# A spectral mixing layer with a two-layer MLP: two more Strassen blocks, a new order inside a Strassen pair, and transform pieces that share ticks

## The chip, the cores and the metric

The kernel runs on one core of a Trainium2 chip. A core has five engines with a queue each: TensorE (PE, matrix products; its weight loads are shown as PEld), VectorE (DVE), ScalarE (ACT), GpSimd (POOL) and SyncE (SP, which issues transfers). Products land in PSUM, eight banks of 128 x 512 float32; ACT and DVE take them out. The metric is the device time of one launch in microseconds (us), the median of the runs.

## The reference, cut to what matters

x is 4 batches of 3008 rows and 256 columns. The output is y = irfft(shrink(rfft(x) W + b)) along the rows, W complex 256 x 256, followed by an MLP over all 12032 rows: silu(y w_in) w_out with 2048 hidden columns.

```
X = np.fft.rfft(x, axis=1)
Yr = Xr @ w_r - Xi @ w_i + b_r ;  Yi = Xr @ w_i + Xi @ w_r + b_i
Yr = sign(Yr) * max(|Yr| - 0.01, 0)      (Yi likewise)
y = np.fft.irfft(Yr + 1j*Yi, n=3008, axis=1)
h = y @ w_in ;  out = (h / (1 + exp(-h))) @ w_out
```

## The kernel before, in words

A DFT of 3008 = 47 x 64 rows is made as two matrix products with a twiddle table between them. Per batch there is a first stage (over the 47; a result of 24 row pairs), a second stage with the mixing product and the shrink (12 steps, each of two rows of the 24), an inverse first stage, and an inverse second stage that makes the rows of the MLP blocks. Between stages the data goes through DRAM (`scr1`, `scr2`).

The MLP works in 24 blocks of 512 rows (the last of 256), and in a block over 16 hidden slices of 128. One hidden slice of one block is a **tick**: `mlp1` makes the hidden slice transposed (six float32r products of 128 x 512: high and low parts of both operands), ACT applies silu and rounds the high part `gh`, DVE makes the low part `gl`, and four **units** (`mlp2`, L675: one 128 x 512 and one 128 x 256 product each) add the slice to the four output accumulators. The units of a tick run two ticks later. PSUM has four accumulators, two banks `h` for `mlp1`, and two banks `d0` and `d1` that everything else takes in turn.

In the blocks of `FAST` (13 to 22) two ticks make a **pair**: the 2x2 form of Strassen-Winograd needs seven half products (three matmuls of 128 x 256 each, `fast_product`, L608) in place of eight. `fast_one` starts a pair in the even tick, `fast_more` goes on in the odd tick, `fast_two` ends it in the next even tick, after the next pair's `fast_one`. A pair holds two banks, `px` and `py`, out of three. `fast_bank` hands a bank out again only when its readers are done.

The transforms of batches 1 to 3 lie between: each tick can hold one transform step, run after `mlp1` and ahead of the tick's units. A planner in plain Python (L930 to L998) gives each step a tick number. The steps are: `i2` and `i2_ends` (inverse second stage of a block, three ticks per block, one PSUM bank); `u3_step` (**U**: the even halves run second stage `s2_3` and inverse first stage `i1`, the odd halves the mixing product `mix3`; two banks each); and for batches 2 and 3 the first stage in 16 pieces (**S**), each in two parts. `stack_split` (L247) rounds 1024 columns of x to `sx` (ACT, L250) and makes the rest in the upper rows (DVE, L251), one buffer; `stack_product` (L254) runs two products of 128 x 512 into two banks (L260), and per bank ACT copies the low half (L261) and DVE adds it (L262). The order of the steps before the change is written as strings of U and S; a split stands up to two ticks ahead of its product, and never before the product of the piece ahead of it. `fills` (L1005) runs a tick's steps in the order in which they were entered, and then hands stores to SP. Each engine's instructions are issued in program order; semaphores make a reader wait for its writer and a writer for the earlier readers of its buffer.

Of the kernel before, what the change touches and what calls it, by code (L numbers as in the profile page):

```python
# [9 lines left out]
F32 = mybir.dt.float32  # L10
F32R = mybir.dt.float32r
U32 = mybir.dt.uint32
ACTF = mybir.ActivationFunctionType
ALU = mybir.AluOpType
# [4 lines left out]
S, D, DFF, NB = 3008, 256, 2048, 4  # L19
# [7 lines left out]
BLK = 512  # L27
# [5 lines left out]

STACKED = 2

FAST = range(13, 23)

X_BUFS = [0, 1, 2, 3, 4, 5, 6, 0, 1, 2, 3, 4, 0, 2, 1, 0]
BLOCKS = [(c, min(BLK, NT - c)) for c in range(0, NT, BLK)]
# [77 lines left out]
def spectral_mlp_kernel(ctx: ExitStack, tc: tile.TileContext, x, w_r, w_i, b_r, b_i, w_in, w_out, c1, c2, c3, c4, c3f, c5, out):  # L117
    nc = tc.nc
# [21 lines left out]
    tl = None  # L140
# [20 lines left out]
    def flush(n):  # L161
        for dst, src in stores[:n]:
            nc.sync.dma_start(out=dst, in_=src)
        del stores[:n]
# [311 lines left out]
    def i2(i, e):  # L476
# [10 lines left out]
        h, l = xt[i]  # L487
        if i in FAST and e == 0:
            xf[i] = tl.tile([128, 2, BLK], F32, tag="xf", bufs=1, name="xf")
        split_x(i, p[:, q], (slice(None), e, q))  # L490

    def split_x(i, v, q):
        h, l = xt[i]
        nc.scalar.copy(h[q], v)
        if i in FAST:
            nc.scalar.copy(xf[i][q], v)
# [58 lines left out]
    HB = BLK // 2  # L555
    xf, th, tw, fast = {}, {}, {}, []
# [51 lines left out]
    def fast_product(p, i, q, a, b, begins):  # L608

        w = [v[:, a, :] for v in tw[q]] if isinstance(a, int) else \  # L610
            [v[:, a[0], q * 256 + a[1] * 128:q * 256 + a[1] * 128 + 128] for v in win]
        m = [v[:, b, :] for v in th[i]] if isinstance(b, int) else \
            [v[:, b[0], b[1] * HB:(b[1] + 1) * HB] for v in xt[i]]
        for n, (j, k) in enumerate(((0, 0), (1, 0), (0, 1))):
            nc.tensor.matmul(  # L615
                out=p, lhsT=w[j], rhs=m[k], start=(begins and n == 0), stop=(n == 2), skip_group_check=True,
            )
# [7 lines left out]
    def fast_one(i, q):  # L625

        px = fast_bank()
        fast_product(px[:, 0:HB], i, q, (0, 0), (0, 0), True)
        fast_product(px[:, HB:BLK], i, q, 0, 0, False)
        u = tl.tile([128, HB], F32, tag="u", bufs=2, name="u")  # L630
        nc.scalar.copy(u, px[:, 0:HB])
        fast.append([i, q, px, u])

    def fast_more():

        i, q, px, u = fast[-1]
        py = fast_bank()
        fast_product(py[:, 0:HB], i, q, 1, 1, True)
        fast_product(py[:, HB:BLK], i, q, 2, 2, False)
        g = tl.tile([128, 4, HB], F32, tag="gp", bufs=3, name="gp")  # L640
        nc.vector.tensor_tensor(out=u, in0=py[:, 0:HB], in1=u, op=ALU.add)
        nc.vector.tensor_tensor(out=g[:, 3, :], in0=px[:, HB:BLK], in1=u, op=ALU.add)  # L642
        nc.vector.tensor_tensor(out=g[:, 3, :], in0=py[:, HB:BLK], in1=g[:, 3, :], op=ALU.add)
        fast[-1] += [py, g]

    def fast_two():

        i, q, px, u, py, g = fast.pop(0)
        fast_product(px[:, 0:HB], i, q, (1, 0), (1, 0), False)
        fast_product(px[:, HB:BLK], i, q, 3, (1, 1), False)  # L650
        fast_product(py[:, HB:BLK], i, q, (1, 1), 3, False)
        nc.scalar.activation(out=g[:, 0, :], in_=px[:, 0:HB], func=ACTF.Silu)  # L652
        nc.vector.tensor_tensor(out=g[:, 2, :], in0=py[:, HB:BLK], in1=u, op=ALU.add)  # L653
        nc.vector.tensor_tensor(out=g[:, 1, :], in0=px[:, HB:BLK], in1=u, op=ALU.add)  # L654
        nc.scalar.activation(out=g[:, 1, :], in_=g[:, 1, :], func=ACTF.Silu)  # L655

        def parts(r):
            h, l = [tl.tile([128, 2, HB], F32R, tag=f"g{k}", bufs=4, name=f"g{k}") for k in "hl"]
            v = g[:, 2 * r:2 * r + 2, :]
            if r:  # L660
                nc.scalar.activation(out=v, in_=v, func=ACTF.Silu)
            nc.scalar.copy(h, v)  # L662
            nc.vector.tensor_sub(l, v, h)  # L663
            gf[i, 2 * q + r] = tuple(a.rearrange("p a c -> p (a c)") for a in (h, l))
            units.extend((i, 2 * q + r, t) for t in range(BLK // 128))

        parts(0)
        later.append(lambda: parts(1))
# [6 lines left out]
    def mlp2(i, f, t):  # L675
# [31 lines left out]
        if i == LAST:  # L707
            (nc.vector.tensor_copy if t % 2 else nc.scalar.copy)(out=o, in_=a[:, 0:D])
        elif i in FAST:
            w = sb.tile([128, 512], F32, tag="g", bufs=3, name="ow")  # L710
# [64 lines left out]
    with tc.manual_schedule():  # L775
# [156 lines left out]
        def at(t, fn, *args):  # L932
            fill.setdefault(t, []).append((fn, args))

        taken = {9, 25} | set(range(33, len(ticks), NFF))

        def put(t, fn, *args):

            while t in taken:
                t += 1  # L940
            taken.add(t)
            at(t, fn, *args)
            return t

        for i in range(1, len(BLOCKS)):
            t = (16 * i - 15 if i in FAST else 16 * i - 9) if i > 1 else -1
            if i > 1:
                at(t, i2_load, i)
            put(t + 2, i2, i, 0)
            put(t + 4, i2, i, 1)  # L950
            t = put(t + 6, i2_ends, i)
            if i in FAST:
                moving = fast_moving(i)
                for k in range(8):
                    at(t + 1 + k, next, moving, None)
                assert t + 8 < 16 * i
# [11 lines left out]
        def turns(b):  # L968

            for u in range(NU + 3):  # L970
                for half in range(2 if 0 < u <= NU else 1):
                    yield b, u, half

        free, stacked = 24, 18
        for b, order in ((1, "U" * 4 + "UUUUSUUUS" * 3 + "UU" + "S." * 10), (2, "UUSUUSUSUS" * 3 + "USUS" + "USU" * 2 + "UUU"), (3, "U" * 27)):
            todo, split = list(turns(b)), 0
            assert order.count("U") == len(todo) and order.count("S") in (0, 16)
            ready = max(free, stacked + 4)
            for k in range(2):
                at(ready - 2 + k, u_load, b, k)  # L980
            for k in order:
                if k == "U":
                    free = put(max(free, ready), u3_step, *todo.pop(0))
                elif k == "S":
                    while free in taken:
                        free += 1
                    at(max(free - 2, stacked), stack_split, b + 1, split)
                    stacked = put(free, stack_product, b + 1, split)
                    split += 1
                last = free  # L990
                free += 1

        def swap_pools():
            nonlocal tl
# [4 lines left out]
        for q in range(NFF // 2):  # L999
            steps = fast_weights(q)  # L1000
            for k in range(3):
                at(last + 2 + q * 8 // 5 + k, next, steps, None)
        assert last + 1 <= 16 * FAST[0] - 13 and last + 2 + 11 + 2 < 16 * FAST[0] + 12

        def fills(t):  # L1005
            for fn, args in fill.pop(t, []):
                fn(*args)
            flush(1 if t < 12 else 4)

        def run(n):  # L1010
            for v in units[:n]:
                mlp2(*v)
            del units[:n]

        def rest_of_pair():
            while later:
                later.pop(0)()

        first_fast, last_fast = 16 * FAST[0], 16 * (FAST[-1] + 1)
        for t in range(len(ticks) + 1):  # L1020
            i, f = ticks[t] if t < len(ticks) else (LAST, None)
            while deferred:
                deferred.pop(0)()
            if t and ticks[t - 1][0] not in FAST:
                split_g(*ticks[t - 1])
            if i in FAST:
                q = t - first_fast
                if f % 2 == 0:
                    state["fast"] = True
                    fast_one(i, f // 2)  # L1030
                    if q != 2:
                        run(2)
                    if q:
                        fast_two()
                        run(2)
                else:
                    run(1)
                    fast_more()
                    if f != 3:
                        rest_of_pair()  # L1040
                    run(1 if q < 4 else 3)
                    rest_of_pair()
                fills(t)
                continue
            if t == last_fast:
                run(2)
                fast_two()
                run(3)
                rest_of_pair()
            if f is not None:  # L1050
                mlp1(i, f)
            fills(t)
            if last_fast <= t < last_fast + 3:
                run(3 if t == last_fast else 4)
            else:
                run(sum(v[:2] != ticks[t - 1] for v in units))
        run(len(units))
        for k, (dst, src) in enumerate(stores):
            eng = nc.scalar if k % 2 else nc.sync
# [28 lines left out]
```

## Time and profile before

| | us |
|---|---|
| median of 3 runs (lowest, highest) | 1353.45 (1353.04, 1359.64) |
| profiled execution, its time | 1355.36 |
| profiled execution, its span | 1353.6 |
| PE busy in the span | 1340.7 (99%) |
| DVE, ACT, POOL busy | 845.2, 800.5, 214.8 |
| transforms end (last inverse step, tick 183) | at about 797 |
| first Strassen block (tick 208) | at 868.5 |

The span runs from the first to the last instruction; the run's time holds the launch as well. PE is busy from the first to the last tick, so its own instructions are read by the distance from one start to the next: a matmul's shown duration overlaps the next one.

### The profile page before, as it was taken

The numbers are of one execution on the slowest core, as the hardware profiler recorded it, in microseconds if no ns is written. First come the engines' busy times: TensorE is split into PE (matmuls) and PEld (weight loads), VectorE is DVE, ScalarE is ACT, GpSimd is POOL, SyncE is SP. The second block draws the span as 40 slices with busy tenths as digits, with TensorE's granted clock in tenths as the row PEclk, the third lists the DMA queues.
The fourth block names the chain that finished last, engine by engine and source line by source line (L and its number), as shares of the span: only waits on it lengthen the run. The fifth ranks groups of instructions, "written<-read, shape, count | busy, mean of one in ns | idle before, by whom it ended". The sixth has DMA issues, their size and how long they took to land.

```text
span 1353.6 us, 22051 instructions
## 1 busy us (share of the span) xinstructions
PE 1340.7 (99%) x8309; PEld 1184.6 (88%) x8309; DVE 845.2 (62%) x1608; ACT 800.5 (59%) x1646; POOL 214.8 (16%) x312
## 2 busy tenths in 40 slices
PE   8999999999999999999999999999999999999998
PEld 4977888888888888888888888899999999999998
DVE  3767757575665767675556656366666666666663
ACT  5546555565676656565554545466666666666665
POOL 2001002121111212121111100122122112212200
PEclk9999999999999999999999999999999999999999
DMA  8876514241434435341433121001100100110001
GB/s 264 260 223 182 137 47 131 73 124 49 121 101 129 120 92 153 76 123 54 119 90 111 50 67 28 7 22 39 28 3 27 40 28 1 28 40 17 1 17 24
DMA packets 72762, 109.85 MB, mean 81 GB/s; under 512 B 8400, under 2 KB 54224, under 8 KB 72656
## 3 DMA queue, kind: packets, MB, share of 16 engines
q1 hardware_dynamic: 58537, 79.07, 20.6%
q0 software_dynamic: 10544, 25.68, 7.4%
q10 hardware_dynamic: 3575, 3.70, 0.9%
q8 instruction: 65, 1.06, 0.3%
q14 instruction: 41, 0.34, 0.1%
HBM read 70.93 MB, written 37.49 MB: 80 GB/s over the span
## 4 chain that ended last, share of the span: by engine, by line
PE 92%; DMA 3%; issue 2%; ACT 1%; DVE 1%; POOL 0%; SPq 0%; DVEq 0%; POOLq 0%; ACTq 0%
PE acc L692 24%; PE h L534 22%; PE h L615 14%; PE acc L696 12%; PE mix L382 6%; PE i L472 3%; PE s L357 2%; PE i L430 2%; PE mix L321 2%; PE s L260 1%; PE acc L687 1%; DMA scr<-s1o 1%; DMA scr<-i1o 1%; PE i2e L472 1%; PE i L427 1%
## 5 line engine op out<-in xcount | busy, mean ns | idle before, releaser
L692 PE MATMUL acc<-wout,gh 128*128 128x512 f32 x1472 | 543.2, 400 | 0.0
L696 PE MATMUL acc<-wout,gl 128*128 128x256 f32 x1472 | 413.0, 281 | 0.2 <-DVE gl L551 0.2
L534 PE MATMUL h<-xt,win 128*128 128x512 f32 (+1 forms) x1344 | 337.5, 386 | 0.0
L692 PEld LDWEIGHTS acc<-wout,gh 128*128 128x128 f32 x1472 | 277.7, 189 | 50.3 <-ACT ww L759 0.3
L541 ACT ACTIVATE g<-h 128x512 f32<-128x512 f32 (+2 forms) x225 | 130.8, 582 | 264.2 <-PE h L534 262.6
L696 PEld LDWEIGHTS acc<-wout,gl 128*128 128x128 f32 x1472 | 278.8, 189 | 4.6 <-DVE gl L551 0.5
L534 PEld LDWEIGHTS h<-xt,win 128*128 128x128 f32 x1344 | 232.2, 188 | 47.2 <-DVE xt L498 0.4
L551 DVE TENSOR_TENSOR gl<-g,gh 128x512 fp32r<-128x512 f32 (+2 forms) x225 | 150.9, 673 | 74.8 <-ACT gh L550 73.5
L663 DVE TENSOR_TENSOR gl<-gp,gh 128x512 fp32r<-128x512 f32 x160 | 117.1, 732 | 102.0 <-ACT gh L662 102.0
L550 ACT CAST gh<-g 128x512 fp32r<-128x512 f32 (+2 forms) x225 | 136.1, 605 | 1.4
L662 ACT CAST gh<-gp 128x512 fp32r<-128x512 f32 x160 | 99.3, 620 | 5.1
L402 DVE TENSOR_TENSOR y<-q,mix 64x256 f32<-64x256 f32 x144 | 60.3, 419 | 58.9 <-PE mix L382 55.0
L389 POOL TENSOR_TENSOR q<-q,bias 128x256 f32<-128x256 f32 x36 | 26.5, 737 | 406.4 <-ACT q L388 406.4
L615 PE MATMUL h<-xt,win 128*128 128x256 f32 x480 | 86.0, 288 | 0.1
L615 PEld LDWEIGHTS h<-xt,win 128*128 128x128 f32 x480 | 68.0, 189 | 7.1 <-DVE gp L642 0.6
L652 ACT ACTIVATE gp<-h 128x256 f32<-128x256 f32 x80 | 30.7, 384 | 73.2 <-PE h L615 73.2
L615 PE MATMUL h<-th,sw_h 128*128 128x256 f32 x240 | 71.0, 296 | 0.5 <-DVE gp L654 0.4
L655 ACT ACTIVATE gp<-gp 128x256 f32<-128x256 f32 x80 | 33.4, 417 | 62.8 <-DVE gp L654 62.8
L653 DVE TENSOR_TENSOR gp<-h,u 128x256 f32<-128x256 f32 x80 | 33.9, 424 | 54.6 <-PE h L615 54.6
L615 PE MATMUL h<-tl,sw_h 128*128 128x256 f32 x240 | 67.8, 282 | 0.0
L615 PE MATMUL h<-th,sw_l 128*128 128x256 f32 x240 | 67.7, 282 | 0.0
L262 DVE TENSOR_TENSOR s1o<-s,s1o 48x512 f32<-48x512 f32 x64 | 41.0, 678 | 32.3 <-ACT s1o L261 32.3
(171 smaller groups left out, 2302.1 us busy)
## 6 DMA issues: line engine op xcount, KB each, us to landing
a<-scr SPq DMA_DIRECT2D x48, 256.0 KB
x_sb<-in_x_dram POOLq DMA_DIRECT2D x64, 188.0 KB, 3.5
gin<-scr SPq DMA_DIRECT2D x30, 384.0 KB
t<-in_c_dram POOLq DMA_DIRECT2D x36, 256.0 KB, 3.1
scr<-i1o SPq DMA_DIRECT2D x36, 256.0 KB
t<-in_c_dram SPq DMA_DIRECT2D x48, 128.0 KB
scr<-s1o SPq DMA_DIRECT2D x32, 192.0 KB
scr<-s1o SPq DMA_DIRECT2D x13, 384.0 KB
```

Source lines behind the costliest of these rows:

```text
L382: nc.tensor.matmul(out=out, lhsT=x_[:, e, c, :], rhs=m[:, e, :], start=(n == 0), stop=(n == 5))
L402: nc.vector.tensor_tensor(out=y[64 * i:64 * i + 64, r, :], in0=q[rows, i, :], in1=pv[rows, i, :], op=op,)
L472: nc.tensor.matmul(out=p[:, o:o + m], lhsT=g_t[b, j // 4][:, q:q + 128], rhs=c4_sb[:, p0:p0 + m], start=True, stop=True,)
L534: nc.tensor.matmul(out=p[:, :n], lhsT=w[:, e, f * 128:(f + 1) * 128], rhs=v[:, e, :n], start=(m == 0), stop=(m == 5),)
L541: nc.scalar.activation(out=g[:, q], in_=p[:, q], func=ACTF.Silu)
L550: nc.scalar.copy(gh[:, q], g[:, q])
L551: nc.vector.tensor_sub(gl[:, q], g[:, q], gh[:, q])
L615: nc.tensor.matmul(out=p, lhsT=w[j], rhs=m[k], start=(begins and n == 0), stop=(n == 2), skip_group_check=True,)
L662: nc.scalar.copy(h, v)
L663: nc.vector.tensor_sub(l, v, h)
L692: nc.tensor.matmul(out=a, lhsT=gh[:, q], rhs=wout[:, f].rearrange("p a c -> p (a c)"), start=begins, stop=False,)
L696: nc.tensor.matmul(out=a[:, D:2 * D], lhsT=gl[:, q], rhs=wout[:, f, 0, :], start=False, stop=ends,)
```

## The change

Blocks 11 and 12 become Strassen blocks too. Inside a pair, the half products change places: `fast_one` makes products 0 and 1, `fast_more` the plain product (0,0) and product 2, `fast_two` product 3 first and then the plain ones; the copy `u` is made in `fast_more`, and the sum that frees `px` follows right behind product 3. The units are laid out otherwise among the calls (`run`), eight per pair as before.

The planner is new. It goes tick by tick, puts an S piece where two or three ticks have passed since the last one and else the next U step, and lets an S piece share a tick with `i2` or `i2_ends`: its product is then entered at tick + 0.5, behind the tick's units. The split of the next piece is entered at whole ticks, at the earliest in the tick of the last product. The last U step moves from tick 183 to tick 162.

```
-FAST = range(13, 23)
+FAST = range(11, 23)
...
     def fast_one(i, q):
         px = fast_bank()
-        fast_product(px[:, 0:HB], i, q, (0, 0), (0, 0), True)
-        fast_product(px[:, HB:BLK], i, q, 0, 0, False)
+        fast_product(px[:, 0:HB], i, q, 0, 0, True)
+        fast_product(px[:, HB:BLK], i, q, 1, 1, False)
...
     def fast_more():
+        i, q, px = fast[-1]
+        py = fast_bank()
+        fast_product(py[:, 0:HB], i, q, (0, 0), (0, 0), True)
+        fast_product(py[:, HB:BLK], i, q, 2, 2, False)
+        nc.scalar.copy(u, py[:, 0:HB])
+        nc.vector.tensor_tensor(out=u, in0=px[:, HB:BLK], in1=u, op=ALU.add)
+        nc.vector.tensor_tensor(out=g[:, 3, :], in0=px[:, 0:HB], in1=u, op=ALU.add)
         nc.vector.tensor_tensor(out=g[:, 3, :], in0=py[:, HB:BLK], in1=g[:, 3, :], op=ALU.add)
...
     def fast_two():
-        fast_product(px[:, 0:HB], i, q, (1, 0), (1, 0), False)
-        fast_product(px[:, HB:BLK], i, q, 3, (1, 1), False)
+        fast_product(px[:, 0:HB], i, q, 3, (1, 1), False)
+        nc.vector.tensor_tensor(out=g[:, 1, :], in0=px[:, 0:HB], in1=u, op=ALU.add)
+        fast_product(py[:, 0:HB], i, q, (1, 0), (1, 0), False)
         fast_product(py[:, HB:BLK], i, q, (1, 1), 3, False)
-        nc.scalar.activation(out=g[:, 0, :], in_=px[:, 0:HB], func=ACTF.Silu)
+        nc.scalar.activation(out=g[:, 1, :], in_=g[:, 1, :], func=ACTF.Silu)
+        nc.scalar.activation(out=g[:, 0, :], in_=py[:, 0:HB], func=ACTF.Silu)
...
+            shared.add(put(t + 2, i2, i, 0))
+            shared.add(put(t + 4, i2, i, 1))
             t = put(t + 6, i2_ends, i)
+            shared.add(t)
...
-        for b, order in ((1, "U" * 4 + "UUUUSUUUS" * 3 + "UU" + "S." * 10), ...
+        while steps:
+            if t not in taken or t in shared:
+                b = steps[0][0]
+                ready = b in stacked and t >= stacked[b] + (3 if b > 1 else 0)
+                apart = 2 if t in shared or not ready else 3
+                if pieces_left and t >= done + apart and pieces_left[0][0] <= b + 1:
+                    at(max(t - 2, done), stack_split, *pieces_left[0])
+                    at(t + 0.5 * (t in shared), stack_product, *pieces_left[0])
+                    done = t
...
+                elif ready and t not in shared:
...
+                    at(t, u3_step, *steps.pop(0))
...
                 if f % 2 == 0:
                     fast_one(i, f // 2)
-                    if q != 2:
-                        run(2)
+                    run(2)
                     if q:
                         fast_two()
-                        run(2)
+                        run(2 if q > 2 else 0)
                 else:
-                    run(1)
                     fast_more()
                     if f != 3:
                         rest_of_pair()
-                    run(1 if q < 4 else 3)
+                    run(2 if q < 4 else 4)
                     rest_of_pair()
...
                 run(sum(v[:2] != ticks[t - 1] for v in units))
+            fills(t + 0.5)
```

Twelve of the 32 S pieces share a tick now (at 41, 43, 45, 57, 59, 61, 91, 93, 105, 107, 109 and 121). On ACT, around the second piece of batch 2 before (tick 42; `gh` and `g` belong to the MLP ticks, `xt` to `i2`, `s1o` to the S piece, `xh` and `xs` to the next U step), the rows are these; the split of this piece stands well ahead, the split of the next one well behind.

```order
L494 CAST xt_2532<-i_2534 128x376 [waits PE_49]
L550 CAST gh<-g 128x512 [waits Activation_49]
L541 ACTIVATE g<-h 128x512 [waits DVE_49,PE_49]
L261 COPY s1o<-s_2563 48x512 [waits PE_49]
L261 COPY s1o<-s_2567 48x512 [waits PE_49]
L550 CAST gh<-g 128x512 [waits Activation_49]
L541 ACTIVATE g<-h 128x512 [waits DVE_49,PE_49]
```

On ACT now, around the same piece (tick 41, then tick 42), the next piece's split `sx` stands between `i2`'s rounding and this piece's two copies.

```order
L494 CAST xt_2532<-i_2534 128x376 [waits PE_49]
L250 CAST sx<-x_sb_72 111x1024 [waits DMASW6_49,DMASW5_49,PE_49]
L261 COPY s1o<-s_2553 48x512
L261 COPY s1o<-s_2557 48x512
L550 CAST gh<-g 128x512 [waits Activation_49]
L541 ACTIVATE g<-h 128x512 [waits DVE_49,PE_49]
L365 CAST xh<-s_2582 128x2x256 [waits PE_49]
```

The split writes the one `sx` buffer, which the piece's two products read; the wait on PE in its row is the one on the second of these products. On DVE now, in the same two ticks, its subtraction stands ahead of the two adds that free the banks.

```order
L551 TENSOR_TENSOR gl<-g,gh 128x512 [waits Activation_49]
L498 TENSOR_TENSOR xt_2533<-i_2534,xt_2532 128x376 [waits Activation_49]
L251 TENSOR_TENSOR sx<-x_sb_72,sx 47x1024 [waits DMASW6_49,Activation_49]
L262 TENSOR_TENSOR s1o<-s_2553,s1o 48x512 [waits Activation_49]
L262 TENSOR_TENSOR s1o<-s_2557,s1o 48x512 [waits Activation_49]
L551 TENSOR_TENSOR gl<-g,gh 128x512 [waits Activation_49]
```

On PE now (end of tick 41, begin of tick 42) the piece stands behind the units, and only the six `mlp1` products lie between it and the next U step, which writes the same two banks.

```order
L692 MATMUL acc<-wout,gh 128x512
L696 MATMUL acc<-wout,gl 128x256
L260 MATMUL s_2553<-sx,c_sb 128x512
L260 MATMUL s_2557<-sx,c_sb 128x512
L534 MATMUL h<-xt_1818,win_83 128x512
L534 MATMUL h<-xt_1818,win_84 128x512
L534 MATMUL h<-xt_1819,win_83 128x512
L534 MATMUL h<-xt_1818,win_83 128x512
L534 MATMUL h<-xt_1818,win_84 128x512
L534 MATMUL h<-xt_1819,win_83 128x512
L357 MATMUL s_2582<-t_2273,a 128x2x64 x4
```

Before, the piece stood ahead of its tick's four units, and `i2` held the next tick. The same order, split ahead of the shared piece's copies and a U step in the tick behind, stands at ticks 41, 43, 57, 59, 91, 105 and 107; at the other five shared pieces no split lies in between.

## Rows read from the trace of the kernel before

**Rows 1.** The page, parts 1 and 2: busy time, granted clock.

```profile
PE 1340.7 (99%) x8309; PEld 1184.6 (88%) x8309; DVE 845.2 (62%) x1608; ACT 800.5 (59%) x1646; POOL 214.8 (16%) x312
PEclk9999999999999999999999999999999999999999
```

**Rows 2.** Waits of PE: line, releaser, us in total, times, longest.

```profile
PE i L472 <- DMA gin<-scr: 3.7, 2, 2.7
```

**Rows 3.** Timeline of PE, ticks and pairs: start, length, what, count.

```profile
854.59 1.55 PE L534 MATMUL h<-xt,win 128*128 128x512 f32 x6
...
865.73 0.63 PE L534 MATMUL h<-xt,win 128*128 128x512 f32 x2
...
1077.07 0.52 PE L615 MATMUL h<-xt,win 128*128 128x256 f32 x3
...
1082.42 0.52 PE L615 MATMUL h<-xt,win 128*128 128x256 f32 x3
...
1093.20 0.52 PE L615 MATMUL h<-xt,win 128*128 128x256 f32 x3
```

**Rows 4.** Timeline at three places where a Strassen product starts late.

```profile
871.97 0.28 PE L615 MATMUL h<-tl,sw_h 128*128 128x256 f32 x1
...
872.30 0.59 PE L615 MATMUL h<-xt,win 128*128 128x256 f32 x3
...
938.31 0.41 DVE L654 TENSOR_TENSOR gp<-h,u 128x256 f32<-128x256 f32 x1
...
938.77 0.39 PE L615 MATMUL h<-th,sw_h 128*128 128x256 f32 x1 [0.21 <-DVE gp L654]
...
939.00 0.28 PE L615 MATMUL h<-th,sw_l 128*128 128x256 f32 x1
...
1319.95 0.28 PE L696 MATMUL acc<-wout,gl 128*128 128x256 f32 x1
...
1320.15 0.61 PE L615 MATMUL h<-xt,win 128*128 128x256 f32 x3
```

**Rows 5.** Groups by line: busy us, mean ns of one, idle before.

```profile
L250 ACT CAST sx<-x_sb 111x1024 fp32r<-111x1024 f32 x32 | 33.6, 1050 | 0.0
L251 DVE TENSOR_TENSOR sx<-x_sb,sx 47x1024 fp32r<-47x1024 f32 x32 | 42.7, 1335 | 27.5 <-ACT sx L250 27.5
L261 ACT COPY s1o<-s 48x512 f32<-48x512 f32 x64 | 34.2, 583 | 0.8
L262 DVE TENSOR_TENSOR s1o<-s,s1o 48x512 f32<-48x512 f32 x64 | 41.0, 678 | 32.3 <-ACT s1o L261 32.3
L631 ACT COPY u<-h 128x256 f32<-128x256 f32 x80 | 30.1, 376 | 22.2 <-PE h L615 21.3
L642 DVE TENSOR_TENSOR gp<-h,u 128x256 f32<-128x256 f32 x80 | 34.0, 424 | 2.7
```

**Rows 6.** Timeline around the first S piece (tick 37).

```profile
227.38 0.62 PE L260 MATMUL s<-sx,c_sb 111*128 111x512 f32 x2
...
227.79 0.60 ACT L541 ACTIVATE g<-h 128x512 f32<-128x512 f32 x1
227.85 0.39 PE L692 MATMUL acc<-wout,gh 128*128 128x512 f32 x1
...
228.42 1.07 ACT L261 COPY s1o<-s 48x512 f32<-48x512 f32 x2
...
229.03 1.28 DVE L262 TENSOR_TENSOR s1o<-s,s1o 48x512 f32<-48x512 f32 x2 [0.41 <-ACT s1o L261]
```

**Rows 7.** Timeline from batch 2's last S piece to its first load.

```profile
416.67 0.63 PE L260 MATMUL s<-sx,c_sb 111*128 111x512 f32 x2
...
419.42 0.30 SPq L163 DMA_DIRECT2D scr<-s1o  x1
...
422.17 0.38 SPq L291 DMA_DIRECT2D a<-scr  x1
```

**Rows 8.** The page, part 6: a load of 256 KB, us to landing.

```profile
t<-in_c_dram POOLq DMA_DIRECT2D x36, 256.0 KB, 3.1
```

More of the change, by code (lines that the diff above doesn't have):

```diff
@@ L627, in fast_one @@
         px = fast_bank()
-        fast_product(px[:, 0:HB], i, q, (0, 0), (0, 0), True)
-        fast_product(px[:, HB:BLK], i, q, 0, 0, False)
-        u = tl.tile([128, HB], F32, tag="u", bufs=2, name="u")
[L631 to L639, printed above, removed]
+        fast_product(px[:, 0:HB], i, q, 0, 0, True)
@@ L640, in fast_more @@
+        fast_product(px[:, HB:BLK], i, q, 1, 1, False)
+        fast.append([i, q, px])
+    def fast_more():
+        i, q, px = fast[-1]
+        py = fast_bank()
+        fast_product(py[:, 0:HB], i, q, (0, 0), (0, 0), True)
+        fast_product(py[:, HB:BLK], i, q, 2, 2, False)
+        u = tl.tile([128, HB], F32, tag="u", bufs=2, name="u")
         g = tl.tile([128, 4, HB], F32, tag="gp", bufs=3, name="gp")
-        nc.vector.tensor_tensor(out=u, in0=py[:, 0:HB], in1=u, op=ALU.add)
-        nc.vector.tensor_tensor(out=g[:, 3, :], in0=px[:, HB:BLK], in1=u, op=ALU.add)
+        nc.scalar.copy(u, py[:, 0:HB])
+        nc.vector.tensor_tensor(out=u, in0=px[:, HB:BLK], in1=u, op=ALU.add)
+        nc.vector.tensor_tensor(out=g[:, 3, :], in0=px[:, 0:HB], in1=u, op=ALU.add)
@@ L643, in fast_more @@
         nc.vector.tensor_tensor(out=g[:, 3, :], in0=py[:, HB:BLK], in1=g[:, 3, :], op=ALU.add)
-        fast[-1] += [py, g]
+        fast[-1] += [u, py, g]
     def fast_two():
         i, q, px, u, py, g = fast.pop(0)
-        fast_product(px[:, 0:HB], i, q, (1, 0), (1, 0), False)
-        fast_product(px[:, HB:BLK], i, q, 3, (1, 1), False)
+        fast_product(px[:, 0:HB], i, q, 3, (1, 1), False)
+        nc.vector.tensor_tensor(out=g[:, 1, :], in0=px[:, 0:HB], in1=u, op=ALU.add)
+        fast_product(py[:, 0:HB], i, q, (1, 0), (1, 0), False)
@@ L651, in fast_two @@
         fast_product(py[:, HB:BLK], i, q, (1, 1), 3, False)
-        nc.scalar.activation(out=g[:, 0, :], in_=px[:, 0:HB], func=ACTF.Silu)
+        nc.scalar.activation(out=g[:, 1, :], in_=g[:, 1, :], func=ACTF.Silu)
+        nc.scalar.activation(out=g[:, 0, :], in_=py[:, 0:HB], func=ACTF.Silu)
         nc.vector.tensor_tensor(out=g[:, 2, :], in0=py[:, HB:BLK], in1=u, op=ALU.add)
-        nc.vector.tensor_tensor(out=g[:, 1, :], in0=px[:, HB:BLK], in1=u, op=ALU.add)
-        nc.scalar.activation(out=g[:, 1, :], in_=g[:, 1, :], func=ACTF.Silu)
@@ L935, in spectral_mlp_kernel @@
         taken = {9, 25} | set(range(33, len(ticks), NFF))
+        shared = set()
         def put(t, fn, *args):
@@ L948, in spectral_mlp_kernel @@
                 at(t, i2_load, i)
-            put(t + 2, i2, i, 0)
-            put(t + 4, i2, i, 1)
+            shared.add(put(t + 2, i2, i, 0))
+            shared.add(put(t + 4, i2, i, 1))
             t = put(t + 6, i2_ends, i)
+            shared.add(t)
             if i in FAST:
@@ L972, in turns @@
                     yield b, u, half
[L974 to L991, printed above, removed]
+        steps = [v for b in range(1, NB) for v in turns(b)]
+        pieces_left = [(b, q) for b in range(STACKED, NB) for q in range(16)]
+        stacked, last, begun = {1: 18}, 24, set()
+        done = 36
+        t = 24
+        while steps:
[7 more added lines that the diff above has]
+                    done = t
+                    if pieces_left.pop(0)[1] == 15:
+                        stacked[max(stacked) + 1] = t
+                elif ready and t not in shared:
+                    if b not in begun:
+                        begun.add(b)
+                        for k in range(2):
+                            at(t - 2 + k, u_load, b, k)
+                    at(t, u3_step, *steps.pop(0))
+                    last = t
+                taken.add(t)
+            t += 1
         def swap_pools():
@@ L1007, in fills @@
                 fn(*args)
-            flush(1 if t < 12 else 4)
+            if t == int(t):
+                flush(1 if t < 12 else 4)
         def run(n):
```

## The prediction

> **What bounds the kernel now.** I read the page's busy shares first, then what PE waited for, then the distances between PE's starts in the timeline. The reader should see in [rows 1] that PE is busy 99% of the span at the full clock, and in [rows 2] that its longest wait in all is 3.7 us, at the start of the first MLP block. So a saving elsewhere is worth nothing unless it removes work or a wait from PE, and every wait put on PE is paid in full. Two yardsticks come from [rows 3]. Four ordinary ticks without a transform take 865.73 - 854.59 = 11.14 us: 2.785 a tick, half of it (1.39) the six products of `mlp1`, half the four units (0.35 each), 5.57 for two ticks. A Strassen pair takes 5.35 (1077.07 to 1082.42) when nothing is late, and 5.39 in the two pairs after it (10.78 to 1093.20).
>
> The 0.04 is a wait that busy time hides. In [rows 4] DVE's sum L654 ends at 938.72, PE starts the next pair's `fast_more` 0.05 later, and the matmul behind that one comes 0.23 after it where 0.12 is usual: a late bank costs the wait and then 0.1 for the restart. Over the ten Strassen blocks I went through the start distances of all L615 matmuls: 63 are longer than usual by 25 ns or more and do not stand behind an inverse piece; together 4.97 us, the first at 871.97 to 872.30, the last at 1319.95 to 1320.15. Most of it is the bank that L654 frees.
>
> **Part 1, two more Strassen blocks.** 16 pairs go from 5.57 to 5.35: 16 x 0.22 = 3.5 us saved, all on PE. The seven products take 21 matmuls at 0.12 = 2.52, against twelve at 1.39 / 6 = 0.232, or 2.78; the rest of the difference is eaten by the units, a little slower in Strassen ticks. What comes with it (the extra copy for the differences, their POOL work, the sums of the weights on DVE) lies in ticks that hold no U step any more, as it did for block 13, where PE shows no wait before 871.97.
>
> The Trainium skill's page "TensorE: Matmul & The Clock Gate", section "Back-to-back issue gap", gives a warm matmul N/2.4 + 2.5 ns, 216 for 512 columns and 109 for 256, so a pair would save 0.30 and the 16 pairs 4.7 us. The rows show 0.232 and 0.12, so the measurement decides; by the page the sum below would be 1.2 us lower.
>
> **Part 2, the order inside a pair.** Before, the bank that `fast_more` takes is freed by the second of two sums behind `fast_two`, with only three units (1.06 us) in between, and that is late again and again. Now product 3 comes first, its sum (0.42, [rows 5]) follows at once, and six matmuls and two units (1.42) lie between product 3's end and the next `fast_more`: drained 0.16 after the next start, plus 0.03, 0.42 and 0.05 makes 0.66, so 0.76 in hand. The new chain is `u`: the copy (0.38) now waits for the plain product in `fast_more`, three sums follow it, and product 3 of the next tick needs the second. On DVE a part's low half (0.7) may stand ahead: about 1.5 us after the end of `fast_more` on PE. Four units, `fast_one`'s six matmuls and two more units last 2.85, so 1.3 in hand. I take 4.5 of the 4.97 as saved. From both sides: all of it and nothing more, 5.0; nothing of it, or a loss of 0.04 in each of 96 pairs (+4), if ACT is late by more than the 1.3 us.
>
> **Part 3, the shared S pieces.** Products, copies, sums and transfers stay the same in number; PE's work does not change. What changes is how close the next user of the two banks stands. An S piece used to have four units and a whole `mlp1` behind it (2.8 us) before the next step's first product; behind the units only `mlp1` is left, 1.39 us. Count from T, the start of `mlp1` behind the piece. In [rows 6] the piece's two products start at 227.38 and end at 228.00, 0.15 after the next matmul's start (227.85). At the five shared pieces without a split, ACT copies the first bank from about T to T + 0.55 (0.58, [rows 5]) and DVE's sum ends near T + 1.26: PE comes at T + 1.39 and finds it free, with 0.1 in hand; the second bank has 0.3. Cost nothing; if that cover goes, up to 0.3 each.
>
> At the other seven (ticks 41, 43, 57, 59, 91, 105, 107) the order in the section on the change puts the next piece's split ahead of the copies on ACT and ahead of the sums on DVE, and this split cannot start before the piece's second product has read `sx`. Then: ACT's cast from T + 0.19 to T + 1.24 (1.05, [rows 5]); DVE's subtraction from T + 1.27 to T + 2.6 (1.34); meanwhile ACT's copies; the first sum from there to T + 3.25 (0.68, less the overlap by which two such sums take 1.28 in [rows 6]); PE 0.05 later, T + 3.3, and 0.1 for the restart [rows 4]. PE had come at T + 1.39: 2.0 us lost. The second sum ends at T + 3.9, before PE has done the 0.7 to 0.8 us of work on the first bank, so it costs nothing more. In each of the seven the next tick holds a U step whose first product takes that bank. 7 x 2.0 = **14.0 us**. From both sides: nothing (if the copies overtook the split), and 2.5 each if the sums were late for PE's second bank too, 17.5. I take 14.0, since each link has a measured length.
>
> Queued behind the waiting cast on ACT are the copies, the `gh` of this tick and the next silu. `gh` is wanted two ticks later and the silu's bank one tick later, so only the two banks are paid for. Behind them on SP is the store of the piece; nothing reads it before the batch's 16 pieces are done.
>
> In the trace ACT keeps its issue order at an S piece: in [rows 6] the first bank was full at about 227.8, but the copy starts at 228.42, behind the silu issued ahead of it (227.79, 0.60 long). The skill's page "PSUM — Partial Sum Buffer", section "Engine vs sequencer instructions", says that the queues of ScalarE and VectorE are strict FIFO. It speaks against this change: by it all seven waits are paid; if a copy could overtake the cast, the time would be the first rival's.
>
> **Part 4, the denser plan.** Batch 2's last piece is now at tick 76 and its first U step at 79, before 88 and 92. In [rows 7] the piece starts at 416.67, its store is issued at 419.42 and the first load at 422.17; [rows 8] has 3.1 us for a load of that size, so it lands 8.6 us after the piece's start, by estimate. From the piece to the U step there are now 0.5 + 1.4 of units, a tick with `i2_ends` (3.3), a tick with a piece (3.3) and 1.4: 9.9 us. Hidden, with 1.3 in hand. The other close neighbours (U after U, unshared S after U, U after S) stand in the old plan too, where no PE wait of any length follows them. I put 0.5 us on this part, between 0 and 3.
>
> **The sum**, on the profiled execution: 1353.6 - 3.5 - 4.5 + 14.0 + 0.5 = 1360.1 for the span. That is +6.5 us; the profiled run's own 1355.36 is 1.9 above the median and I hold that apart, so the median goes from 1353.45 to about **1359.9**.
>
> **Rivals.** (a) The seven waits do not reach PE: the copies go first, or the banks turn out to be other ones. For it: PE's waits in this stretch are nil today. Against it: the order rows and ACT's issue order in [rows 6]. Then 1353.45 - 3.5 - 4.5 = 1345.5, faster. (b) The pair's new order doesn't pay: `u` is on the way of product 3, and where ACT is late by more than 1.3 us (four copies of accumulators at a block's end) PE waits again, as much as it did. Then 1353.45 - 3.5 + 14.0 + 0.5 = 1364.5, slower by 0.8%. For it: the old order's waits cluster where ACT is loaded; against it: margins of 0.76 and 1.3 where the old one was below zero. (c) The split's wait is half covered: DVE takes the sums first or the subtraction overlaps them, and PE waits for the copy alone (cast to T + 1.24, copy 0.5, sum 0.7: T + 2.5, so 1.1 each). Then 1353.45 - 8.0 + 7.7 + 0.5 = 1353.7, no change. Against it the DVE rows.
>
> **How the numbers follow.** What a measurement of this kernel can tell from no change is about 0.5%, 6.8 us: faster means below 1346.7, slower above 1360.2. Forecast 0.66, its own range 1356.5 to 1363, which lies about 0.4 of the time above 1360.2 (0.28) and else within (0.38). (a) 0.11, mostly faster (0.09). (b) 0.09, slower. (c) 0.12, the same, and 0.02 for anything else. Slower 0.37, same 0.53, faster 0.10. The range 1351 to 1364.5 holds the forecast, most of (c) and half of (b).
>
> **What would show it.** Right: in ticks 42, 44, 58, 60, 92, 106 and 108 PE idles before the first product of a U step (L357 or L382), released by DVE's sum in `stack_product`, 1.9 us each; ACT's cast in front of it waits for PE. Pairs take 5.35 throughout, and the first pairs of block 11 start without the 0.3 us gap that block 13 shows. The transforms end at tick 162. Wrong: no idle time at the seven places (then a); PE waits for the sums behind `u` (then b); PE waiting there for ACT's copy alone (then c); or a wait for a load at the first U step of batch 2.

## The result and the profile after

Six runs of the changed kernel have a median of 1364.72 us (1363.07 to 1366.68), six of the kernel before 1353.54. The ratio of comparable runs is 1.0075, with a 95% interval of 1.0060 to 1.0089: **10.2 us slower** (8.1 to 12.0), 1363.6 on the median before. The profiled execution took 1365.58, its span 1363.8.

The page of the changed kernel answers to [rows 1] with

```profile
PE 1335.0 (98%) x8453; PEld 1187.3 (87%) x8453; DVE 891.3 (65%) x1680; ACT 806.9 (59%) x1690; POOL 223.1 (16%) x336
```

PE is busy for 5.7 us less than before and the span is 10.2 longer. So the time is not in PE's work; PE stands. The view of its waits, which had nothing over 3.7 us in [rows 2], says where (waiting line, releaser, us in all, times, longest):

```profile
PE s L357 <- issue: 7.1, 4, 1.8
PE mix L382 <- DVE s1o L262: 5.5, 3, 1.8
PE i L472 <- DMA gin<-scr: 3.9, 2, 2.9
PE i L427 <- DVE y L328: 2.1, 1, 2.1
...
PE s L357 <- DMA a<-scr: 1.3, 1, 1.3
```

Four waits at L357 and three at L382, 1.8 us each: the seven places of Part 3. Four are put down to "issue", which means that the view names no releaser there. What stood in front of them is seen in the timeline of the first place, the end of tick 41 and the next U step (answers to [rows 6]; start, length, what, idle time before):

```profile
248.79 0.63 PE L260 MATMUL s<-sx,c_sb 111*128 111x512 f32 x2
249.26 1.55 PE L534 MATMUL h<-xt,win 128*128 128x512 f32 x6
249.46 1.05 ACT L250 CAST sx<-x_sb 111x1024 fp32r<-111x1024 f32 x1 [1.41 <-PE s L260]
250.53 1.06 ACT L261 COPY s1o<-s 48x512 f32<-48x512 f32 x2
250.54 1.22 DVE L251 TENSOR_TENSOR sx<-x_sb,sx 47x1024 fp32r<-47x1024 f32 x1 [1.91 <-ACT sx L250]
...
251.79 1.28 DVE L262 TENSOR_TENSOR s1o<-s,s1o 48x512 f32<-48x512 f32 x2
...
252.58 0.68 PE L357 MATMUL s<-t,a 128*128 128x128 f32 x4 [1.77 <-issue]
```

T is 249.26. ACT is idle for 1.41, until the piece's second product has read `sx`, then casts from T + 0.20; the two copies, whose banks are full, stand behind that. DVE is idle for 1.91 and then subtracts from T + 1.28. The first of the two sums that start at 251.79 (0.68, [rows 5]) is over near 252.47, and PE starts 0.1 behind it, at T + 3.32 (0.15 behind it at the three places of L382). The matmul behind a late start comes 0.07 later than it usually does; this is called the restart below.

The last row of the waits is Part 4. The timeline from the last S piece of batch 2 to its first U step (answers to [rows 7]):

```profile
392.88 0.63 PE L260 MATMUL s<-sx,c_sb 111*128 111x512 f32 x2
...
394.31 1.28 DVE L262 TENSOR_TENSOR s1o<-s,s1o 48x512 f32<-48x512 f32 x2 [2.31 <-ACT s1o L261]
395.62 0.30 SPq L163 DMA_DIRECT2D scr<-s1o  x1
...
398.44 0.38 SPq L291 DMA_DIRECT2D a<-scr  x1
...
399.37 0.43 SPq L291 DMA_DIRECT2D a<-scr  x1
...
404.06 0.68 PE L357 MATMUL s<-t,a 128*128 128x128 f32 x4 [1.31 <-DMA a<-scr]
```

The view of the chain that ended last, followed back from there, is the store and then the load (start, length, what):

```profile
395.62 2.68 DMA scr<-s1o
...
398.44 5.48 DMA a<-scr
```

The load landed 5.48 us after its issue. The trace also records when the last part of the same load, from the same queue, landed in the kernel before: 2.61 after its issue at 422.17, and PE did not wait for it. The DMA engines were about half busy while it ran, and nearly full while it ran in the changed kernel (the last but one number; first before, then changed):

```profile
422.17:424.78 2.61, 2.61 (x15) 2.18 (x14) 0.86 (x2) 0.84 (x3) 0.00 (x0) 1.00 0.54 166
398.44:403.92 5.48, 4.31 (x21) 3.28 (x19) 2.57 (x4) 3.21 (x6) 0.43 (x1) 1.00 0.98 284
```

Two stretches sum it up (window, length, PE busy and count ...; granted clock, DMA share, GB/s). The first runs from tick 32 to the first Strassen block, the second over the twelve Strassen blocks:

```profile
205.89:792.26 586.37, 572.51 (x3389) 502.30 (x3387) 395.69 (x709) 346.66 (x686) 111.26 (x174) 1.00 0.37 100
792.26:1332.54 540.28, 539.77 (x3796) 502.83 (x3795) 356.85 (x726) 332.70 (x748) 96.00 (x132) 1.00 0.08 23
```

586.37 - 572.51 = 13.9 us without PE in the transforms, 0.5 in the Strassen blocks, and the full clock in both. Before, the same view has no idle PE in the transforms and 453.85 for ten Strassen blocks (its first stretch ends where block 12 starts):

```profile
204.32:821.24 616.92, 616.92 (x3633) 542.90 (x3631) 397.10 (x715) 364.05 (x718) 102.67 (x166) 1.00 0.36 98
868.52:1322.37 453.85, 453.29 (x3160) 419.09 (x3159) 287.59 (x602) 282.90 (x620) 89.23 (x108) 1.00 0.08 22
```

Tick 32 comes at 201.48 to 205.89 in the eight profiled executions of this study, at 204.31 and 203.83 in two of one and the same kernel. That start scatters by more than most parts of this change are worth, so below the length **from tick 32 to the end of the span** stands beside each timed ratio:

| kernel | ratio to before (95%) | from tick 32, us | against before |
|---|---|---|---|
| before | | 1353.6 - 204.32 = 1149.28 | |
| changed | 1.0075 (1.0060, 1.0089) | 1363.8 - 205.89 = 1157.91 | +8.6 |
| split behind the piece | 0.9964 (0.9949, 0.9980) | 1349.3 - 204.31 = 1144.99 | -4.3 |
| the same, once more | 0.9953 (0.9939, 0.9968) | 1348.7 - 203.83 = 1144.87 | -4.4 |
| cast ahead, subtraction behind | 1.0033 (1.0021, 1.0046) | 1356.2 - 202.79 = 1153.41 | +4.1 |
| pair order alone | 0.9975 (0.9964, 0.9987) | 1349.1 - 203.86 = 1145.24 | -4.0 |
| split behind, blocks 13 to 22 | 0.9987 (0.9975, 1.0000) | 1349.0 - 201.48 = 1147.52 | -1.8 |
| split behind, loads earlier | 0.9951 (0.9937, 0.9965) | 1346.4 - 202.39 = 1144.01 | -5.3 |

### The profile page after: what moved, and what is told of

Its sections match the earlier page's. It is cut to its first block, busy times and chain, and to the rows that moved or that the text cites. A ratio compares the mean times of both kernels' runs of the same rounds, so it can differ in the third digit from the quotient of the medians.

```text
span 1363.8 us, 22616 instructions
## 1 busy us (share of the span) xinstructions
PE 1335.0 (98%) x8453; PEld 1187.3 (87%) x8453; DVE 891.3 (65%) x1680; ACT 806.9 (59%) x1690; POOL 223.1 (16%) x336
## 4 chain that ended last, share of the span: by engine, by line
PE 91%; DMA 4%; issue 2%; ACT 2%; DVE 1%; POOL 0%; SPq 0%; ACTq 0%; DVEq 0%; POOLq 0%
PE acc L692 24%; PE h L534 18%; PE h L615 17%; PE acc L696 12%; PE mix L382 6%; PE i L472 3%; PE s L357 2%; PE i L430 2%; PE mix L321 2%; DMA scr<-s1o 1%; PE s L260 1%; DMA scr<-i1o 1%; PE acc L687 1%; DMA w<-in_moe_w_in_dram 1%; PE i2e L472 1%
## 5 line engine op out<-in xcount | busy, mean ns | idle before, releaser
L534 PE MATMUL h<-xt,win 128*128 128x512 f32 (+1 forms) x1152 | 287.9, 385 | 0.0
L541 ACT ACTIVATE g<-h 128x512 f32<-128x512 f32 (+2 forms) x193 | 111.5, 578 | 207.8 <-PE h L534 206.6
L534 PEld LDWEIGHTS h<-xt,win 128*128 128x128 f32 x1152 | 199.3, 188 | 40.4 <-DVE xt L498 0.4
L663 DVE TENSOR_TENSOR gl<-gp,gh 128x512 fp32r<-128x512 f32 x192 | 137.8, 718 | 42.1 <-ACT gh L662 42.1
L551 DVE TENSOR_TENSOR gl<-g,gh 128x512 fp32r<-128x512 f32 (+2 forms) x193 | 128.8, 668 | 46.8 <-ACT gh L550 45.1
L662 ACT CAST gh<-gp 128x512 fp32r<-128x512 f32 x192 | 119.1, 620 | 6.1
L550 ACT CAST gh<-g 128x512 fp32r<-128x512 f32 (+2 forms) x193 | 116.3, 603 | 1.0
L615 PE MATMUL h<-xt,win 128*128 128x256 f32 x576 | 101.0, 284 | 0.5 <-DVE gp L650 0.5
L655 DVE TENSOR_TENSOR gp<-h,u 128x256 f32<-128x256 f32 x96 | 40.8, 425 | 72.6 <-ACT gp L654 72.6
L615 PEld LDWEIGHTS h<-xt,win 128*128 128x128 f32 x576 | 81.9, 189 | 7.0 <-DVE gp L650 2.0
L650 DVE TENSOR_TENSOR gp<-h,u 128x256 f32<-128x256 f32 x96 | 40.6, 423 | 47.3 <-PE h L615 46.7
L251 DVE TENSOR_TENSOR sx<-x_sb,sx 47x1024 fp32r<-47x1024 f32 x32 | 43.7, 1366 | 41.2 <-ACT sx L250 41.2
```

Source lines behind the costliest of these rows:

```text
L534: nc.tensor.matmul(out=p[:, :n], lhsT=w[:, e, f * 128:(f + 1) * 128], rhs=v[:, e, :n], start=(m == 0), stop=(m == 5),)
L541: nc.scalar.activation(out=g[:, q], in_=p[:, q], func=ACTF.Silu)
L550: nc.scalar.copy(gh[:, q], g[:, q])
L551: nc.vector.tensor_sub(gl[:, q], g[:, q], gh[:, q])
L615: nc.tensor.matmul(out=p, lhsT=w[j], rhs=m[k], start=(begins and n == 0), stop=(n == 2), skip_group_check=True,)
```

## The experiments

**Where the split stands.** Only the place of the split changes at a shared tick; the plan stays.

```
-                    at(max(t - 2, done), stack_split, *pieces_left[0])
+                    at(max(t - 2, behind), stack_split, *pieces_left[0])
                     at(t + 0.5 * (t in shared), stack_product, *pieces_left[0])
-                    done = t
+                    done, behind = t, t + 0.5 * (t in shared)
```

> The changed kernel with one thing different: at a shared tick the split of the next piece is entered behind the shared piece, so that ACT has the two copies ahead of the cast and DVE the two sums ahead of the subtraction. Plan, pairs and blocks stay. Theory (the split in front of the copies costs 7 waits of 1.95 us and 0.07 each for the restart): 14 us go, 1364.7 becomes about 1350.7, and no PE wait over 0.3 us is left at ticks 42, 44, 58, 60, 92, 106, 108. Rival (mlp1 alone, 1.4 us, is too short to empty two banks, split or not): the waits shrink to 0.3 to 0.6 each and the time is 1353 to 1355. Rival (the cast, now later, makes gh late): the copies' time is given back at the units two ticks on, 1358 or more.

Measured: 1350.3 us, ratio 0.9964, faster than before; from tick 32 on 12.9 less than the changed kernel. The same place in the timeline:

```profile
247.22 0.63 PE L260 MATMUL s<-sx,c_sb 111*128 111x512 f32 x2
247.65 1.07 ACT L261 COPY s1o<-s 48x512 f32<-48x512 f32 x2 [1.18 <-PE s L260]
247.68 1.55 PE L534 MATMUL h<-xt,win 128*128 128x512 f32 x6
248.26 1.28 DVE L262 TENSOR_TENSOR s1o<-s,s1o 48x512 f32<-48x512 f32 x2 [1.21 <-ACT s1o L261]
248.61 1.05 ACT L250 CAST sx<-x_sb 111x1024 fp32r<-111x1024 f32 x1
249.07 1.09 PE L357 MATMUL s<-t,a 128*128 128x128 f32 x8
```

T is 247.68, and the U step starts at T + 1.39 with no idle time: the first sum (0.68) is over at T + 1.26. So `mlp1` alone is cover enough for the first bank, and the first rival falls; the late `gh` (the second) shows nowhere. But next to nothing is in hand: PE starts 0.13 behind the sum, and where it waited it started 0.06 to 0.15 behind one. At the ten shared places where the sum ends at T + 1.26 the U step's second matmul comes 0.14 to 0.18 behind its first; at the two where it ends at T + 0.93, and behind unshared pieces, it is 0.11 or 0.12. That is 0.4 us in all. The seven waits are gone from the list; the wait for the load is still there, and two new ones stand at L260:

```profile
PE s L357 <- DMA a<-scr: 1.1, 1, 1.1
...
PE s L260 <- ACT rest L514: 0.6, 2, 0.3
```

At ticks 45 and 109 the shared piece stands behind `i2_ends`, and its second product wants the bank that `i2_ends` leaves last. By the distance of the starts the two places lose 0.46 and 0.49 us. In the changed kernel PE had stood for 1.9 us in the tick before, and no wait showed at either place: of the 14.2 us that the seven places cost there (1.92 to 1.98 each, and 0.07 for the restart), 0.95 is handed back at the next place in line. With it 13.2 is left, and 12.9 came.

**Which half of the split.** ACT's cast stays ahead of the copies, and DVE's subtraction moves behind the sums.

```
-        nc.vector.tensor_sub(sx[64:64 + RR, :], t[64:64 + RR, :], sx[64:64 + RR, :])
-        x_t[b, q] = sx
+        x_t[b, q] = sx, t
+    def stack_rest(b, q):
+        sx, t = x_t[b, q]
+        nc.vector.tensor_sub(sx[64:64 + RR, :], t[64:64 + RR, :], sx[64:64 + RR, :])
+        x_t[b, q] = sx
...
+                    at(max(t - 2, behind), stack_rest, *pieces_left[0])
```

> The changed kernel with only DVE's half of the split moved: the cast stays ahead of the shared piece's copies on ACT, the subtraction goes behind the piece's sums on DVE. The chain left is cast (to T + 1.27, T the start of mlp1 behind the piece), copy 0.53, sum 0.68 from about T + 1.8: the bank is free at T + 2.5, PE came at T + 1.4. Theory (cast and subtraction stand in one chain and each pays its own length): 1.1 us at each of the seven places in place of 1.95, so 6 us of the 14 go, about 1358.5. Rival (ACT's cast alone does the harm, DVE's subtraction lies beside ACT's copies): no change, 1364. Rival (only the subtraction does it): as if the whole split had moved, 1350.7.

Measured: ratio 1.0033, 1357.9 on the median before; from tick 32 on 4.5 less than the changed kernel. PE's waits (its lines lie four lower here, so L361 is L357 and L266 is L262) and the first place:

```profile
PE s L361 <- DVE s1o L266: 4.3, 4, 1.1
...
PE mix L386 <- DVE s1o L266: 3.2, 3, 1.1
```

```profile
246.15 1.55 PE L538 MATMUL h<-xt,win 128*128 128x512 f32 x6
246.35 1.05 ACT L250 CAST sx<-x_sb 111x1024 fp32r<-111x1024 f32 x1 [1.41 <-PE s L264]
247.42 1.06 ACT L265 COPY s1o<-s 48x512 f32<-48x512 f32 x2
248.04 1.28 DVE L266 TENSOR_TENSOR s1o<-s,s1o 48x512 f32<-48x512 f32 x2 [2.52 <-ACT s1o L265]
...
248.78 0.94 PE L361 MATMUL s<-t,a 128*128 128x128 f32 x6 [1.07 <-DVE s1o L266]
```

Seven waits of 1.07 in place of 1.8: PE starts at T + 2.63 in place of T + 3.32 and T + 1.39. Cast and subtraction stand in one chain; the cast costs 1.24 a place and the subtraction 0.7 more, since half of it lies beside the copies. Both other theories fall. The gain was 4.5 where 6 was expected: PE is 1.24 late at each place and not 1.1, since the sum ends at T + 2.57 and not at T + 2.5, and PE starts 0.06 behind it; and the restart, 0.10 here, I had not counted.

**The pair's order alone.** The three functions and the layout of the units of the changed kernel, in the kernel before (blocks 13 to 22, old planner).

> The kernel before with only the new order inside a Strassen pair (the three functions and the layout of the units), blocks 13 to 22, old planner. Forecast: 4.5 of the 4.97 us of late starts go, 1353.5 becomes 1349.0. By the trace of the changed kernel, where 12 Strassen blocks show 4 or 5 late starts of about 0.08 each: 10 blocks lose about 3.7, 1349.8. Rival (the old order's small waits were hidden elsewhere, or the new order's units wait as much): 1353.5.

Measured: ratio 0.9975; from tick 32 on 4.0 less. The transforms take what they took, the ten Strassen blocks 4.00 less:

```profile
203.86:820.69 616.83, 616.83 (x3632) 543.18 (x3631) 396.92 (x715) 363.77 (x718) 102.36 (x166) 1.00 0.36 98
867.97:1317.82 449.85, 449.45 (x3160) 418.75 (x3159) 296.14 (x602) 275.91 (x621) 78.56 (x108) 1.00 0.08 22
```

The margins of Part 2 can be read in one pair:

```profile
1092.16 0.42 DVE L650 TENSOR_TENSOR gp<-h,u 128x256 f32<-128x256 f32 x1 [0.77 <-PE h L615]
...
1093.38 0.52 PE L615 MATMUL h<-xt,win 128*128 128x256 f32 x3
...
1094.30 0.37 ACT L640 COPY u<-h 128x256 f32<-128x256 f32 x1 [0.34 <-PE h L615]
...
1095.16 0.42 DVE L642 TENSOR_TENSOR gp<-h,u 128x256 f32<-128x256 f32 x1
...
1096.93 0.27 PE L615 MATMUL h<-xt,sw_h 128*128 128x256 f32 x1
```

The sum behind product 3 (L650) is over at 1092.58, and `fast_more` takes the bank at 1093.38: 0.80 in hand. The sum that product 3 of the next tick waits for (L642) is over at 1095.58, product 3 starts at 1096.93: 1.35 in hand. Beside the starts behind inverse pieces, the kernel before has 63 late ones (25 ns or more), together 5.0 us, and this one 16, together 1.8: 3.2 of the 4.0 are these starts, and most of the rest lies between the units. The two longest that are left stand at 873.67 (0.34) and 1285.19 (0.38), in the first and the last Strassen block; the others are of 0.11 or less.

**The two blocks alone.** The split behind the piece, and `FAST = range(13, 23)`.

> The changed kernel with the split behind the shared piece (as in the first of these runs) and with blocks 13 to 22 by Strassen in place of 11 to 22: beside the first run it prices the two blocks alone. Theory: 16 pairs of 0.22 us, 3.5 us more than the first run, about 1354.2. Rival (a pair gives 0.30, as by the columns alone): 4.7 more. Rival (the blocks' setting up, weights and differences, costs what they give): no difference.

Measured: ratio 0.9987 against 0.9964, 3.1 us by the two ratios. By the trace of the first experiment the twelve blocks take 540.32; here blocks 13 to 22 take 449.81 and 11 and 12, from 773.90 to 867.98, 94.08:

```profile
867.98:1317.79 449.81, 449.41 (x3161) 418.73 (x3159) 296.22 (x602) 275.94 (x621) 78.57 (x108) 1.00 0.08 22
```

543.89 - 540.32 = 3.6 us for 16 pairs, 0.22 each. So the rival with 4.7 falls, and no cost of the blocks' setting up shows. The two intervals alone would not tell 3.1 from 4.7; the trace does. From tick 32 this kernel is 1147.52 and the pair order alone 1145.24. They differ in the planner and the sharing only, so these still cost 2.3 us with the split out of the way: 0.95 at the two L260 waits, 0.4 at batch 2's first U step (0.2 of wait and the restart; the list has it at 0.2 here and 1.1 in the first experiment), 0.4 at the second matmuls of the ten places without anything in hand, and 0.5 spread over lines, which no run here takes apart.

**The load at batch 2's first U step.** A batch's first U step stands four ticks behind its last piece in place of three, and batch 2's last piece comes one slot earlier. The split is behind the piece as above.

```
-                ready = b in stacked and t >= stacked[b] + (3 if b > 1 else 0)
+                ready = b in stacked and t >= stacked[b] + (4 if b > 1 else 0)
                 apart = 2 if t in shared or not ready else 3
+                if pieces_left and pieces_left[0] == (2, 15):
+                    apart = 1
```

> The split behind the shared piece, as in the first experiment, and the first U step of a batch four ticks behind its last S piece in place of three, with batch 2's last piece one slot earlier (behind tick 75's units, one tick after the piece before). Everything else as in the changed kernel, transforms still end at tick 162. Theory (PE's 1.1 to 1.3 us at batch 2's first U step is store, then load, one behind the other; the piece's sums now end half a tick, 1.4 us, earlier): the wait shrinks to 0 to 0.2, the time is 1.2 below the first experiment's, about 1349.1. Rival (the load waits for transfer engines that are full at that time, not for the store): the wait stays near 1 us and the time at 1350.3. Rival (the last piece, now one tick behind the one before, is late itself): a new PE wait at tick 75 of 0.5 or more.

> The first experiment's kernel (split behind the shared piece) once more on the chip of this comparison: 1350.3, with the wait of 1.1 to 1.3 us at batch 2's first U step and no other PE wait over 0.6 us behind tick 24.

Measured: 1348.19 us, ratio 0.9951, beside 1349.6 and 0.9953 for the first experiment's kernel: by time the two can't be told apart. The first experiment's kernel shows the wait of 1.1 for the load again, and no other of over 0.33 behind tick 24, as expected. In the new one the wait is gone by the trace (the list of PE's waits has no load at L357), and from tick 32 on 0.9 is saved:

```profile
381.69 1.28 DVE L262 TENSOR_TENSOR s1o<-s,s1o 48x512 f32<-48x512 f32 x2 [1.21 <-ACT s1o L261]
...
385.82 0.38 SPq L291 DMA_DIRECT2D a<-scr  x1
...
391.75 0.49 PE L357 MATMUL s<-t,a 128*128 128x128 f32 x3
```

The load is issued 2.85 behind the end of the sums, as in the changed kernel (398.44 - 395.59), and PE comes 5.9 later without a wait; where it waited it came 5.6 behind the issue (changed kernel) and 5.45 (first experiment, 389.42 to 394.87). Two things moved. From the store's issue to the point at which PE wants the load there are 1.8 us more than in the first experiment's kernel beside it, and by the records of landing the load took 4.33 us in place of 5.25. The 1.8 alone is more than the wait, which by the distance of the starts was 1.2, so the first theory (store, then load) holds. The rival (full transfer engines) is not out as the reason why the load is long: at 4.33 it is still longer than the 2.61 of the kernel before. No wait shows at tick 75. The gain was 0.9 of 1.2, and a start that was not late before stands at 457.91: it comes 0.45 behind the one in front of it, within a U step, where it came 0.16 behind in the first experiment. This kernel has the lowest time and the shortest stretch from tick 32 on, and it beats the one before by 0.5% (0.35 to 0.63).

## Why the prediction came out as it did

The direction and the mechanism of the main term were right, the size was short: +6.5 forecast, +10.2 (8.1 to 12.0) measured, +8.6 from tick 32 on. The time lies at the upper end of the range (1364.5; 1363.6 by the ratio, 1364.72 by the plain median), and beyond the forecast's own range, which ended at 1363. I gave most of the chance to less than half a percent, and it was three quarters.

- **Part 1**, -3.5: -3.6 by the pair of runs with and without blocks 11 and 12.
- **Part 2**, -4.5: -4.0. The margins were 0.80 and 1.35 where 0.76 and 1.3 were worked out. The term was over-sized: 1.8 us of late starts stay in the new order, the longest in the first and the last Strassen block. So one sign did not come true: in the changed kernel a matmul near the start of block 11 (798.07) comes 0.45 late, where no gap of 0.3 was to be. Pairs with nothing else in them take 5.33, as forecast (5.35).
- **Part 3**, +14.0: seven late starts of 1.92 to 1.98 us, and 0.07 each for the restart, 14.2. What the Trainium skill's page "PSUM — Partial Sum Buffer", section "Engine vs sequencer instructions", says of ScalarE's and VectorE's queues, strict FIFO, the trace agrees with: the two copies start at T + 1.27, behind a cast that waited, and at T - 0.03 in the first experiment, where no cast stands in front of them. The chain was right link by link (cast at T + 0.20 for T + 0.19, subtraction at T + 1.28 for T + 1.27, PE at T + 3.32 for T + 3.3), at the seven ticks named. Two small errors cancel in it: the subtraction took 1.22 for 1.34, and PE started 0.1 to 0.15 behind the sum for 0.05. The other five shared pieces show no wait, as forecast; but the 0.1 in hand that I gave their first bank is not there, and with the split out of the way two of them (ticks 45 and 109) cost 0.95, for the bank of `i2_ends` and not the U step's, which I had not looked at.
- **Part 4**, +0.5: +1.5 (a start 1.47 late, and the restart). **This is the step that failed in size.** I gave a load 3.1 us from issue to landing, after [rows 8], and found 1.3 in hand. The rest of the chain came as forecast (5.56 from the piece's start to the load's issue, for 5.5), but the load took 5.48, and the margin was gone. [rows 8] is a load from another queue, but that is not the fault: the very load, in the kernel before, took 2.61. In the old plan it took 2.61 and 2.64 us (the kernel before and the pair order alone); in the new plan, in six traces, 4.33 to 5.48. So the denser plan made the load longer, and that I had put at nothing; the pair order alone and the run with blocks 13 to 22, which differ in the planner and the sharing only, have 2.64 and 4.40. A wait for a load at this step had been named as a sign of being wrong, and it came. The share of the DMA engines that was busy while it ran was 0.54 and 0.47 in the old plan and 0.90 to 1.07 in the new one (the view can go over 1).
- The rest: the parts sum up to 14.2 + 1.5 - 3.6 - 4.0 = 8.1 of the 8.6 from tick 32 on. The profiled execution also started 1.6 later (one wait at L427, 2.1, long before any changed tick). The timed runs lie 1.6 above the 8.6, within their interval; whether a part of that is real stays open.

Rival (a) fell at the seven waits. Its time, 1345.5, is nearly what the kernel with split and load mended shows (1353.45 x 0.9951 = 1346.8). Rival (b) fell with the pair order alone. Rival (c) described not this kernel but the second experiment, where PE waits for cast, copy and sum: it starts 1.24 late at each place, for the 1.1 worked out.

## What to carry to other kernels

When a planner moves a step next to the user of its buffer, list everything that is entered between the step and that user on the in-order engines that free the buffer; an instruction that waits there holds up all behind it, however early its own result is wanted. Price such a wait link by link from the rows of the operations; that came out within 2% here (14.2 for 14.0). And do not give a load one landing time, not even the one that it has now in its place: the same load took 2.61 us here before the plan was changed and up to 5.48 after. With 1.3 us in hand on a chain of 9, look at which other transfers the new plan puts beside it.

## What the runs showed of the hardware

The load's time is the one surprise. The store lands 2.68 us after its issue (395.62 to 398.30 in the changed kernel), SP issues the load 0.14 behind that, and where PE waited it started 0.14 behind the load's landing. Of one form, the 48 loads of 256 KB that SP issues (`a<-scr`), the landing times in the kernel before go from 2.61 to 8.26 us, while the page's median for another 256 KB load was 3.1 before and 3.7 now. The load that decided took 2.61 and 2.64 us with the DMA engines about half busy, and 4.33 to 5.48 with them nearly full. Within the new plan a higher share does not go with a longer load (4.40 at 1.07, 5.48 at 0.98), and no run takes single transfers out from beside it; so which of the neighbours makes it longer stays open.
